# Two slots of a streamed grouped projection share one block of pixels and one store

## The chip, the cores and the metric

The kernel runs on one core of a Trainium2 chip. The time is device microseconds of one execution of the whole program. Three runs of the kernel before took 476.24, 476.40 and 476.92 us, the median is 476.4 us. One more execution was taken with the hardware profiler on; the profile lines in this document come from it.

## The reference

The input is an image of 512 x 512 pixels with 192 channels in bfloat16 (100.7 MB). The channels form 4 groups of 48, and each group has its own 48 x 48 matrix. With a kernel size of 1 there is no neighbourhood: every pixel is multiplied, group by group, by its group's matrix.

```python
H = W = 512; G = 4; Cg = 48; C = 192; k = 1
xg = xp.reshape(B, H, W, G, Cg)
out = out + jnp.einsum('bhwgc,gcd->bhwgd', xg, w[0, 0])
return out.reshape(B, H, W, C)
```

So 262,144 pixels of 384 bytes are read once and written once, and each byte takes part in very little arithmetic.

## The kernel before

**Columns and slots.** Pixels lie in SBUF (the on-chip memory of 128 partitions) as "columns": one column is one pixel of 192 channels in each of the 128 partitions. The input ring `xin` and the output ring `xout` each hold 256 columns. The work is cut into slots of 64 columns, each a block of 128 x 64 pixels that is contiguous in DRAM: partition p gets 64 pixels in a row, that is 24,576 contiguous bytes. `plan_pieces` (L79) makes the list. Slot 0 is cut into pieces of 8, 24 and 32 columns (`HEAD`). Slots 6 and 22 (`SHARED_AT`) are "shared": they fill only some of the partitions, 16 rows by SyncE's queue and 44 rows by GpSimd's queue. The last piece has 4 columns.

**Groups and pairs.** Four columns are a group, two groups a pair. For each group TensorE transposes six 128 x 128 blocks from `xin` into PSUM (`transposes`, L250), VectorE copies the transposed blocks of a whole pair to SBUF (L311), TensorE multiplies them with a block-banded weight matrix `wt` (`matmuls`, L264), and ScalarE casts the 128 x 768 result from PSUM into `xout` (L346). TensorE works one pair ahead with its transposes. There are 529 groups, 16 to a full slot.

**Loads.** SyncE issues them (L234), piece by piece in order. Before a piece it waits until TensorE has finished with the part of the ring that the piece will overwrite (`groups_before`, L180, from the counter `mm_done`). With a ring of four slots the load for a slot is issued when the slot four places earlier is about consumed. GpSimd issues its share of the shared slots, and it also passes each load's landing on to TensorE: it waits for the load's semaphore and raises `ready` (L217 to L219), on which TensorE waits before the first transposes of a piece (L253).

**Stores.** ScalarE issues them from a list made ahead of time (L135 to L146). An entry says which piece, which of its columns, and the group at which it ends. A full slot is one store of 64 columns; in the last nine slots (`LATE`) it is two of 32 columns, and the last but one slot is cut into 24, 16, 12 and 12. ScalarE issues a store after the cast of the second group behind the entry's last one (L347: the entry's end must be smaller than the group just cast). Before it casts a group into a place of `xout` that was used 64 groups earlier, it waits for the store that took that place's old contents (`wait_stored`, L342, found through `store_of`).

```python
for g in range(NG):
    if g >= OUT_COLS // 4:
        wait_stored(store_of[g - OUT_COLS // 4])
    wq.wait(mm_done, g + 1)
    ...
    while todo and todo[0][3] < g:
        store()
```

**Who waits for whom.** TensorE's matmuls wait for ScalarE's casts to free the PSUM buffers (`o_left`, L268) and for VectorE's copies (`e_left`, L265). ScalarE waits for TensorE (`mm_done`) and for stores. SyncE waits only for TensorE.

**DMA engines.** A transfer of all 128 partitions is spread over the core's 16 DMA engines, 8 partitions to an engine. Loads, stores and GpSimd's transfers are in three different queues of the same 16 engines.

Of the kernel before, what the change touches and what calls it, by code (L numbers as in the profile page):

```python
# [11 lines left out]
C = GROUPS * CG  # L12
# [12 lines left out]
SLOT = 64  # L25
# [4 lines left out]
LAST_PARTS = (24, 16, 12, 12)  # L30
LOOP = IN_COLS // 4
SHARED_AT = (6, 22)
SYNC, POOL = 0, 1
SHARED = ((0, 16, 4, SLOT, SYNC), (52, 44, 11, SLOT, POOL))
AHEAD = IN_COLS // SLOT - 2
# [5 lines left out]
class Waiter:  # L41

    def __init__(self, eng):
        self.eng = eng
        self.seen = {}
# [14 lines left out]

class Piece:

    def __init__(self, i, slot, g0, size, shares, pix):
        self.i, self.slot, self.size = i, slot, size
        self.at = {IN_COLS: 4 * g0 % IN_COLS, OUT_COLS: 4 * g0 % OUT_COLS}
        self.g0, self.g1 = g0, g0 + size // 4
        self.full = shares is None
        self.blocks = []
        for (r0, rows, parts, cols, queue) in shares or ((0, 128, 1, size, SYNC),):
            self.blocks.append(Block(r0, rows, parts, cols, queue, pix))  # L70
            pix += rows * cols
        self.pix_end = pix
        assert size % 4 == 0 and all(at + size <= cols for cols, at in self.at.items())
# [5 lines left out]
def plan_pieces(npix):  # L79
    few = sum(rows * cols for _, rows, _, cols, _ in SHARED)  # L80
    at = list(SHARED_AT)
    if npix < len(at) * few + 128 * SLOT * (1 + at[-1]):
        at = []
    cols = (npix - few * len(at)) // 128
    assert cols % 4 == 0
    pieces, g, pix, n = [], 0, 0, 0
    while cols:
        if n in at:
            parts = [(SLOT, SHARED)]
        elif n == 0 and cols >= SLOT:  # L90
            parts = [(s, None) for s in HEAD]
        else:
            parts = [(min(SLOT, cols), None)]
        for s, shares in parts:
            pieces.append(Piece(len(pieces), n, g, s, shares, pix))
            cols -= 0 if shares else s
            g, pix = pieces[-1].g1, pieces[-1].pix_end
        n += 1
    assert pix == npix
    return pieces  # L100


def bass_standalone__grouped__vision_kernel(nc, x, w, out):
# [3 lines left out]
    assert npix % 512 == 0, "the pixel count must be a multiple of 512"  # L107

    pieces = plan_pieces(npix)
    piece_of = {g: p for p in pieces for g in range(p.g0, p.g1)}  # L110
    NG = pieces[-1].g1
# [12 lines left out]
    def transfers(ap, ring, p, queue, c0=0, c1=None):  # L124
        at = p.at[ring.shape[1] // C]
        for b in p.on(queue):
            px = ap[b.pix:b.pix + b.rows * b.cols, :]
            e0, e1 = c0, min(c1 or b.cols, b.cols)
            if b.parts == 1:
                view = px.rearrange("(p i) n -> p (i n)", p=b.rows)[:, e0 * C:e1 * C]  # L130
            else:
                view = px.rearrange("(c a i) n -> a c (i n)", a=b.parts, c=b.rows // b.parts)
            yield b, view, ring[b.r0:b.r0 + b.rows, (at + e0) * C:(at + e1) * C]

    stores = []  # L135
    for p in pieces:
        late = pieces[-1].slot - p.slot
        half = p.size // 8 * 4
        parts = (p.size,)
        if p.full and p.size == SLOT and late < LATE:  # L140
            parts = LAST_PARTS if late == 1 else (p.size - half, half)
        c = 0
        for n in parts:
            stores.append((p, c, c + n, p.g0 + (c + n) // 4))
            c += n
# [4 lines left out]
    with ExitStack() as es:  # L150
# [34 lines left out]
        def _(gp):  # L185
# [13 lines left out]
            def pool_dmas(p, ap, ring, inward, done):  # L199
                for b, dram, sbuf in transfers(ap, ring, p, POOL):  # L200
                    turn = (b.engine - cursor[0]) % 16
                    if turn:
                        few = xf[0:turn, 0:128].rearrange("p (a b) -> p a b", a=2)[:, :, 0:32]
                        gp.dma_start(cur[0:turn, turns[0]], few).then_inc(cur_sem, 16)  # L204
                        turns[0] += 1
                    gp.dma_start(*((sbuf, dram) if inward else (dram, sbuf))).then_inc(done, 16)  # L206
                    cursor[0] = (b.engine + b.parts) % 16
# [20 lines left out]
        @block.sync  # L228
        def _(sp):
            wq = Waiter(sp)  # L230
            for p in pieces:
                wq.wait(mm_done, groups_before(p))
                for _, dram, sbuf in transfers(xf, xin, p, SYNC):
                    sp.dma_start(sbuf, dram).then_inc(ld_sem[p.i], 16)  # L234
# [88 lines left out]
        def _(act):  # L323
# [4 lines left out]
            def store():  # L328
                i = len(stores) - len(todo)
                p, c0, c1, g1 = todo.pop(0)  # L330
                for _, dram, sbuf in transfers(of, xout, p, SYNC, c0, c1):
                    act.dma_start(dram, sbuf).then_inc(st_sem[i], 16)
# [49 lines left out]
```

## Time and profile before

| what | value |
|---|---|
| median of three runs | 476.4 us (476.24 to 476.92) |
| the profiled execution | 476.13 us, of which the span from first to last instruction is 474.0 us |
| TensorE matmul busy | 437.0 us (92%) |
| ScalarE busy | 398.3 us (84%), of which 529 casts of 802 ns on average |
| VectorE busy | 254.1 us (54%) |
| mean rate of all DMA over the span | 425 GB/s (201.53 MB) |
| loads of 64 columns | 30 of 3072 KB on SyncE's queue, 35.7 us from issue to landing (median) |
| stores of 64 columns | 22 of 3072 KB on ScalarE's queue, 33.2 us from issue to landing (median) |
| stores of 32 columns | 15 of 1536 KB, 33.9 us (median) |

The first table of a profile page gives for each engine how long it was busy, its share of the span and how many instructions it ran. The row DMA cuts the span into 40 slices and gives in tenths how busy the 16 DMA engines were on average. A line of a DMA queue names the queue, how many packets it moved, how many MB, and what share of the time of 16 engines these packets took. In the list of waits a line reads: who waited, for whom, microseconds in total, how many times, the longest. In an engine's order of time a line gives start, duration, engine, line of the kernel and operation; an engine's name with a q is its instruction queue, which issues DMAs.

### The profile page before, as it was taken

Reading aid. Unit: us, or ns where it says so; the run is one execution under the profiler, and the core shown is the slowest. Engines: PE = TensorE matmul, PEld = TensorE weight load, DVE = VectorE, ACT = ScalarE, POOL = GpSimd, SP = SyncE. Lnnn points to the kernel's source line nnn. Section 1 sums busy time; section 2 is a strip of 40 time slices with the busy share of each in tenths; the row PEclk is TensorE's granted clock in tenths of the full one; section 3 lists DMA queues with packets and bytes.
Section 4 is the critical chain, followed back from the end, with each engine's and each line's share of the span. In section 5 each row is a group of like instructions: output and inputs, shape, how many; then the busy total and the mean of one; then the engine's idle time right before and its main releaser. Section 6 shows DMA issues by size and latency. Waiting matters only on the chain.

```text
span 474.0 us, 14050 instructions
## 1 busy us (share of the span) xinstructions
PE 437.0 (92%) x6358; PEld 394.0 (83%) x6358; DVE 254.1 (54%) x266; ACT 398.3 (84%) x530; POOL 5.9 (1%) x16
## 2 busy tenths in 40 slices
PE   5999999999999999998889859999999999999970
PEld 5898889888898989887779759898889888898850
DVE  2555655555655555564555525655555555655530
ACT  2899989998999989998788848999889998989870
POOL 1001000000000000000000000000000000000000
PEclk9999999999999999999999989999999999999995
DMA  8999999999999999999999999999999999999997
GB/s 360 401 413 442 427 427 431 429 429 429 425 429 432 431 431 429 435 433 431 429 432 431 433 436 431 433 431 431 431 430 433 430 423 430 438 421 427 427 425 331
DMA packets 11981, 201.53 MB, mean 425 GB/s; under 512 B 1744, under 2 KB 2000, under 8 KB 2640
## 3 DMA queue, kind: packets, MB, share of 16 engines
q10 hardware_dynamic: 6584, 98.52, 48.7%
q1 hardware_dynamic: 4936, 98.50, 48.7%
q0 software_dynamic: 448, 4.33, 2.2%
q8 instruction: 8, 0.13, 0.1%
q14 instruction: 5, 0.04, 0.0%
HBM read 100.68 MB, written 100.66 MB: 425 GB/s over the span
## 4 chain that ended last, share of the span: by engine, by line
PE 63%; DMA 31%; issue 1%; ACT 1%; SPq 0%; POOLq 0%; ACTq 0%
PE o_ps L275 37%; PE xT_ps L260 26%; DMA xin<-in_x_dram 23%; DMA out_dram<-xout 9%; ACT xout L346 1%; SPq L234 0%; POOLq L219 0%; ACTq L51 0%
## 5 line engine op out<-in xcount | busy, mean ns | idle before, releaser
L346 ACT CAST xout<-o_ps 128x768 bf16<-128x768 f32 x529 | 397.0, 802 | 60.7 <-PE o_ps L275 50.5
L311 DVE COPY xT_sb<-xT_ps 128x1536 bf16<-128x1536 bf16 x265 | 253.4, 956 | 198.6 <-PE xT_ps L260 198.6
L275 PE MATMUL o_ps<-wt,xT_sb 128*128 128x144 bf16 (+1 forms) x3174 | 294.7, 234 | 5.6 <-ACT xout L346 1.4
L275 PEld LDWEIGHTS o_ps<-wt,xT_sb 128*128 128x128 bf16 x3174 | 213.3, 98 | 45.5 <-ACT xout L346 30.6
L260 PE MATMUL xT_ps<-ident,xin 128*128 128x128 bf16 x3174 | 223.3, 221 | 12.4 <-POOLq L219 11.1
L260 PEld LDWEIGHTS xT_ps<-ident,xin 128*128 128x128 bf16 x3174 | 191.8, 99 | 15.3 <-POOLq L219 12.6
L204 POOL DMA_DIRECT2D cur<-in_x_dram x4 | 2.3, 584 | 321.2 <-PE o_ps L275 161.4
L246 PE MATMUL o_ps<-w_sb,esel 48*128 48x48 bf16 x10 | 0.6, 209 | 4.4 <-DMA w_sb<-in_w_dram 4.4
L246 PEld LDWEIGHTS o_ps<-w_sb,esel 48*128 48x128 bf16 x10 | 0.5, 111 | 4.3 <-issue 4.3
L305 DVE CAST wt<-o_ps 128x480 bf16<-128x480 f32 x1 | 0.7, 658 | 5.0 <-PE o_ps L246 5.0
L346 ACT ACT_TABLE_LOAD x1 | 1.3, 1283 | 1.3 <-PEq L367 1.3
L206 POOL DMA_DIRECT2D xin<-in_x_dram x2 | 1.1, 564 | 0.0
L206 POOL DMA_DIRECT2D out_dram<-xout x2 | 1.1, 559 | 0.0
L190 POOL TENSOR_SCALAR_AFFINE_SELECT esel<-esel 48x272 bf16<-48x272 bf16 x1 | 0.4, 403 | 0.0
L187 POOL MEMSET esel<- 48x272 bf16 x1 | 0.3, 317 | 0.3 <-POOLq L367 0.3
L194 POOL TENSOR_SCALAR_AFFINE_SELECT ident<-ident 128x128 bf16<-128x128 bf16 x1 | 0.3, 282 | 0.0
L188 POOL MEMSET ident<- 128x128 bf16 x1 | 0.2, 198 | 0.0
L367 POOL MEMSET const-float32-0.0<- 128x1 f32 x1 | 0.1, 99 | 0.3 <-issue 0.3
L367 POOL MEMSET const-bfloat16-1.0<- 128x1 bf16 x1 | 0.1, 102 | 0.0
L367 POOL MEMSET const-uint8-127<- 128x1 uint8 x1 | 0.1, 102 | 0.0
L367 POOL MEMSET const-float32-1.0<- 128x1 f32 x1 | 0.1, 99 | 0.0
## 6 DMA issues: line engine op xcount, KB each, us to landing
xin<-in_x_dram SPq DMA_DIRECT2D x30, 3072.0 KB, 35.7
out_dram<-xout ACTq DMA_DIRECT2D x22, 3072.0 KB, 33.2
out_dram<-xout ACTq DMA_DIRECT2D x15, 1536.0 KB, 33.9
out_dram<-xout ACTq DMA_DIRECT2D x2, 1152.0 KB, 17.7
xin<-in_x_dram POOLq DMA_DIRECT2D x2, 1056.0 KB, 19.8
out_dram<-xout POOLq DMA_DIRECT2D x2, 1056.0 KB, 19.3
xin<-in_x_dram SPq DMA_DIRECT2D x1, 1536.0 KB, 8.9
xin<-in_x_dram SPq DMA_DIRECT2D x3, 384.0 KB, 3.2
```

Of the source, the lines that this page charges most:

```text
L187: gp.memset(esel[:], 1.0).then_inc(p0_sem, 1)
L190: gp.affine_select(out=esel[:], in_=esel[:], pattern=[[-1, ECOLS]], compare_op=AluOpType.is_equal, fill=0.0, base=ESHIFT, channel_multipli ...
L194: gp.affine_select(out=ident[:], in_=ident[:], pattern=[[-1, 128]], compare_op=AluOpType.is_equal, fill=0.0, base=0, channel_multiplier=1) ...
L204: gp.dma_start(cur[0:turn, turns[0]], few).then_inc(cur_sem, 16)
L206: gp.dma_start(*((sbuf, dram) if inward else (dram, sbuf))).then_inc(done, 16)
L246: last = pe.matmul(o_ps[:, NOB - 1, col:col + CG], lhsT=esel[:, s0:s0 + 128], rhs=w_sb[:, g, :], start=True, stop=True, skip_group_check=True)
L260: last = pe.transpose(xT_ps[:, g % NXP, i * 128:(i + 1) * 128], xg[:, i * 128:(i + 1) * 128], ident[:])
L275: last = pe.matmul(o_ps[:, v % NOB, c0_:c1_], lhsT=xs[:, i * 128:(i + 1) * 128], rhs=wt[:, WOFF[tc]:WOFF[tc] + (c1_ - c0_)], start=(tc == ...
L305: dve.tensor_copy(wt[:], o_ps[:, NOB - 1, 0:WCOLS]).then_inc(wc_sem, 1)
L311: dve.tensor_copy(xT_sb[pair % NXS][:, 0:n * 2 * UC].rearrange("p (g c) -> p g c", g=n), xT_ps[:, b0:b0 + n, 0:2 * UC]).then_inc(e_left, 1)
L346: act.copy(dst, o_ps[:, v % NOB:v % NOB + 2, 0:UC]).then_inc(o_left, 1)
L367: nc = _bacc.Bacc("TRN2", target_bir_lowering=False, num_devices=1)
```

## The change

Slots 2 to 5 and 8 to 21 are taken two by two. The two slots of a couple no longer are two blocks of 128 x 64 pixels, but share one block of 128 x 128 pixels: partition p holds 128 pixels in a row (49,152 contiguous bytes in DRAM). The first slot's load takes the first 64 of every partition's pixels, the second slot's load the last 64, so that a load's rows still have 24,576 bytes but lie 49,152 bytes apart in DRAM. The two slots are neighbours in `xin` and `xout`, in halves of the ring. They are stored together, by one transfer of 128 columns whose rows are 49,152 contiguous bytes on both sides. This store takes the place of two in ScalarE's list, and its end is that of the second slot. All other pieces stay as they were. On the other engines the instructions and their order stay the same; on ScalarE nine DMA issues go, and the waits for stores are nine fewer.

```diff
+DOUBLE = (2, 4, 8, 10, 12, 14, 16, 18, 20)
...
-    def __init__(self, i, slot, g0, size, shares, pix):
+    def __init__(self, i, slot, g0, size, shares, pix, off=0, width=0):
...
+        self.double = False
...
-        for (r0, rows, parts, cols, queue) in shares or ((0, 128, 1, size, SYNC),):
+        for (r0, rows, parts, cols, queue) in shares or ((0, 128, 1, width or size, SYNC),):
...
+        elif n in DOUBLE and cols >= 2 * SLOT:
+            for off in (0, SLOT):
+                pieces.append(Piece(len(pieces), n + off // SLOT, g, SLOT, None, pix, off, 2 * SLOT))
+                pieces[-1].double = True
+                g = pieces[-1].g1
+            cols -= 2 * SLOT
+            pix = pieces[-1].pix_end
+            n += 2
+            continue
...
-            e0, e1 = c0, min(c1 or b.cols, b.cols)
+            e0, e1 = c0, c1 or p.size
             if b.parts == 1:
-                view = px.rearrange("(p i) n -> p (i n)", p=b.rows)[:, e0 * C:e1 * C]
+                view = px.rearrange("(p i) n -> p (i n)", p=b.rows)[:, (p.off + e0) * C:(p.off + e1) * C]
...
     for p in pieces:
+        if p.double and p.off:
+            continue
+        if p.double:
+            p = Piece(p.i, p.slot + 1, p.g0, 2 * SLOT, None, p.blocks[0].pix)
```

More of the change, by code (lines that the diff above doesn't have):

```diff
@@ L61 @@
 class Piece:
-    def __init__(self, i, slot, g0, size, shares, pix):
-        self.i, self.slot, self.size = i, slot, size
+    def __init__(self, i, slot, g0, size, shares, pix, off=0, width=0):
+        self.i, self.slot, self.size, self.off = i, slot, size, off
         self.at = {IN_COLS: 4 * g0 % IN_COLS, OUT_COLS: 4 * g0 % OUT_COLS}
```

## The prediction

> **What bounds the kernel now.** I read the page first (busy shares, the slices, the DMA queues), then the waits, then the DMA view in three windows, and last ACT's order of time around its store issues.
>
> ```profile
> span 474.0 us, 14050 instructions
> PE 437.0 (92%) x6358; PEld 394.0 (83%) x6358; DVE 254.1 (54%) x266; ACT 398.3 (84%) x530; POOL 5.9 (1%) x16
> DMA  8999999999999999999999999999999999999997
> q10 hardware_dynamic: 6584, 98.52, 48.7%
> q1 hardware_dynamic: 4936, 98.50, 48.7%
> q0 software_dynamic: 448, 4.33, 2.2%
> ```
>
> q1 carries SP's loads, q10 ACT's stores, q0 POOL's transfers. With 0.1% of instruction fetches the shares add up to 99.7%: on average an engine has a packet in work for 472.6 of 474.0 us. PE at 92% looks almost as full, but PE is the faster of the two. ACT's order of time shows its store issues while nothing starves:
>
> ```profile
> 116.08 0.33 ACTq L332 DMA_DIRECT2D out_dram<-xout  x1
> 129.26 0.34 ACTq L332 DMA_DIRECT2D out_dram<-xout  x1
> 142.38 0.34 ACTq L332 DMA_DIRECT2D out_dram<-xout  x1
> ```
>
> A slot (16 groups) is computed in 13.1 to 13.2 us. Its transfers take longer, as the DMA view of 130 to 190 us (only whole 64-column loads and stores), of 366 to 416 us (stores halved to 32 columns) and of 440 to 460 us (such stores, no loads) shows:
>
> ```profile
> DMA packets 1189, 25.89 MB, mean 431 GB/s; under 512 B 135, under 2 KB 135, under 8 KB 135
> q10 hardware_dynamic: 595, 13.05, 50.7%
> q1 hardware_dynamic: 593, 12.83, 49.7%
> ...
> q1 hardware_dynamic: 613, 13.35, 62.1%
> q10 hardware_dynamic: 615, 8.16, 38.3%
> ...
> DMA packets 783, 8.56 MB, mean 428 GB/s; under 512 B 87, under 2 KB 87, under 8 KB 87
> q10 hardware_dynamic: 782, 8.54, 100.7%
> ```
>
> First window: 100.4% of 16 engines' 60 us is 963.8 us; less 135 semaphore packets at 0.009 us (their time in the packet records), over 1053 data packets: 0.914 us for one row of 24,576 bytes. An engine has 8 of a slot's 128 rows, so a slot costs it 16 x 0.914 = 14.6 us, load and store. DMA therefore sets the pace, and what PE gains per slot it later waits. The middle window shows how an engine shares itself: 613 packets of one queue to 615 of the other, though the stores' rows are half as long, so the bytes go 62 to 38. The queues take turns by packet, not by byte. The last window shows that one queue alone keeps the engines full.
>
> ```profile
> ACT xout L346 <- PE o_ps L275: 50.5, 133, 6.8
> PEld xT_ps L260 <- POOLq L219: 12.6, 7, 5.1
> ACT xout L346 <- DMA out_dram<-xout: 1.7, 2, 1.3
> ```
>
> The 12.6 us behind POOL's "ready" are waits for loads (7 times, to 5.1 us). ACT hardly ever waits for a store: 1.7 us.
>
> **The change, part by part.**
>
> *Loads.* Same count, rows, bytes, issue waits; only the pitch of the rows in DRAM is 49,152 instead of 24,576 bytes. No load here has a pitch of twice its row, but the late stores have: halves of 12,288 bytes in rows 24,576 apart. 440 to 460 us gives 322.2 us less 87 x 0.009, over 695 packets: 0.4625 us, and two of them are 0.925, 0.011 above one long row. So a pitch of two rows costs no more than the extra packet. I take 0; ends: nothing gained (an engine is no quicker than 0.914 in any stretch), and 1.2% lost, that same 0.011 of 0.925 charged to pitch: 1.6 us on 18 slots x 8 x 0.914 = 131.6.
>
> *Stores.* Eighteen stores of 64 columns become nine of 128: per engine 144 packets of 24 KB become 72 of 48 KB. What a packet costs beside its bytes is that 0.011 us by the windows; by the medians of the packet records (0.460 for 12 KB, 0.912 for 24 KB) it is 0.008. I take 0.009: a 48 KB packet takes 1.82 us, and 72 x 0.009 = 0.65 us goes. Nine semaphore packets go too: 9 x 0.009 = 0.08. Together 0.73 us, on the path because the engines are never free. Ends: 0, and 72 x 0.011 + 0.08 = 0.87. The nine issues that ACT drops (0.34 us each, 3 us) are beside the path, under DMA.
>
> The Trainium skill, "DMA: Bandwidth & Descriptors", section "Bandwidth", gives a transfer a fixed cost of about 2 us and advises batching; nine transfers fewer would by that be an estimated 18 us. Here that latency lies under other transfers, as the 99.7% shows, so the trace does not bear it out; it is the last rival.
>
> *The first half waits.* A pair's first slot is stored 13.1 us later. No work is lost by this if the engines have loads meanwhile. In 190 to 260 us a load lands 45.3 us after its issue (median), three loads deep; in 95 to 200 us a store lands after 30.8, two deep. Taking one store of 14.6 us out of the mix leaves both the loads and the rest of the last store. Cover gone, it costs up to 13.1 us a pair, but only if no load is outstanding.
>
> *The out ring.* xout holds 256 columns, now four parts in two halves. A pair's store is issued behind the second cast of the next slot and must have landed 31 casts later, before the ring is reused: 31 x 0.82 (13.1/16) = 25.4 us, where one slot's store had 47 casts, 38.5 us, for its 30.8. What a pair needs: turns by packet, 8 x (1.82 + 0.914) = 21.9 us with loads always in between; plus what issue and landing take, 3.2 us for a 384 KB load into idle queues less 8 x 0.12 for its packets, 2.2. That is 24.1 us: it fits by 1.3. When loads hold PE to 14.6 us a slot there are 28.3. If ACT does wait, every later cast is queued behind it, PE's matmuls behind ACT's counter, and SP's next load and POOL's shared transfers behind PE's. Still nothing is lost while DMA has something queued: the last cast ends near 460.3 us and the last store lands at 473.6; a last store alone would need about 5, so a delay of PE up to some 8 us is hidden.
>
> *Loads beside a pair's store* get a third of an engine: 21.9 us for a load instead of 14.6, then 7.3 alone when the store is through. Over a pair that is 29.2 for two loads and two stores, as now, and the ring of four slots has taken landings of 49.0 us. Cost 0.
>
> **Sum.** 476.13 (the profiled execution, 474.0 of span and 2.1 around it) less 0.73 is 475.40. The median of the runs, 476.4, is 0.27 above that execution: 475.7, which is 0.15% less than 476.4.
>
> **Rivals.**
>
> *The 48 KB row goes out as two packets of 24 KB.* Then turns are one to one: 16 x 2 x 0.914 = 29.2 and 2.2 is 31.4 us against 25.4, ACT waits 6 us for each of nine pairs, and nothing is saved on packets. Unstalled, the casts (first at 9.3 us in ACT's order of time, then 33 slots) would end at 9.3 + 33 x 13.1 = 442; with 9 x 6 on that 496, and 5 for the last store 501. The floor is the 474 of DMA. Loads that run dry speed up the stores, so I take the middle, about 487. For it: no row here is longer than 24,576 bytes. Against: each length from 3,072 to 24,576 went out as one packet. It decides as soon as rows are cut. The Trainium skill's "DMA: Bandwidth & Descriptors", section "Queues, rings and completion order", has a contiguous run moved by one descriptor and cuts only rows longer than 64 KiB, which speaks against this rival; no run yet shows a 48 KB row.
>
> *Whole packets, but the store lands late.* If a pair's landing exceeds 27.2 us, then with two casts (1.6) and the issue (0.4) before the next store a pair takes more than 29.2, and loads run dry in the gap. At 28.5 us it is 1.3 x 9 = 11.7, less the 8 hidden: 479.4. For it: POOL's queue takes a third turn beside slots 4-5 and 20-21, and the margin is 1.3. Against: once loads have caught up, the store gets the whole engine.
>
> *The fixed part of each transfer comes out.* Nine times the 2.2 us above, 20 us: about 456. Against: no idle DMA between 2 us and 471 for it to come from.
>
> **How the numbers follow.** About 0.2%, 0.95 us, is what a measurement of this kernel can tell from no change, so the border of "faster" is 475.45. Forecast 0.76; two packets 0.13; late landing 0.10; fixed cost 0.01. The forecast's own range is 474.9 to 476.6: a saving of 0 to 0.87, the 1.6 of pitch against it, and the spread of the three runs (476.24 to 476.92). It lies close to the border: of its 0.76, 0.28 falls faster, 0.45 same, 0.03 slower. With the fixed cost faster is 0.29; with 0.01 of the late landing same is 0.46; the rest of the rivals makes slower 0.25. The range reaches to 479.4, so that only the two packets, the fixed cost and the forecast's edges are out, 2 in 10.
>
> **What would show it.** Right: store packets of 49,152 bytes (1152 data packets fewer on q10), about 1.82 us each; between a pair's store and its landing some 24 to 27 us; bytes on q10 to q1 about two to one while both run; DMA still 9 in all slices but the ends; ACT's wait for stores under 20 us in total. Wrong: stores' packets as many as now, ACT waiting for DMA 6 us at each pair and slices of DMA below 9 after 140 us; or load packets well above 0.92 us, which would be the pitch.

## The result, and the profile after

The changed kernel takes 489.55 us (median of six runs, 485.35 to 492.24) against 476.65 us before (six runs, 475.88 to 476.97). The ratio is 1.0262, 95% interval 1.024 to 1.0285: by the ratio, slower by 12.5 us. The forecast was 475.7, its range 474.9 to 479.4. The profiled execution took 489.66 us, 13.5 more than that of before. Of 48 more executions of the kernel before, taken beside the experiments, seven were slow runs of 489 to 498 us; these and one run of the cut at 112 and 16 columns stay out of every ratio below, and as no trace of the seven was kept, whether the kernel before can lose its time in the same way is open.

From the page of the changed kernel: span, busy times, DMA's share and rate in 40 slices, the DMA queues (packets, MB, share) and the issues (count, KB each, median us to landing):

```profile
span 487.6 us, 14032 instructions
PE 443.0 (91%) x6358; PEld 401.4 (82%) x6358; DVE 254.0 (52%) x266; ACT 398.8 (82%) x530; POOL 5.9 (1%) x16
DMA  8999999999999999999999999999999999999995
GB/s 356 416 401 432 438 452 407 395 448 379 429 429 432 419 391 419 448 401 403 425 431 399 416 405 431 411 425 433 391 401 431 432 426 429 429 429 424 427 399 234
q1 hardware_dynamic: 4936, 98.50, 48.3%
q10 hardware_dynamic: 5288, 98.52, 48.2%
out_dram<-xout ACTq DMA_DIRECT2D x9, 6144.0 KB, 28.0
```

The bytes are those of before, and q10 has 1296 packets fewer: 1152 of data and 144 semaphore packets. So the change did what it says, and a row of 48 KB goes out as one packet. DMA is still shown busy in every slice, but the slices from 70 to 350 us move 379 to 452 GB/s, where before they moved 425 to 436. This is the same row of the page of before:

```profile
GB/s 360 401 413 442 427 427 431 429 429 429 425 429 432 431 431 429 435 433 431 429 432 431 433 436 431 433 431 431 431 430 433 430 423 430 438 421 427 427 425 331
```

The engines are not idle, they are slower. The DMA view of 60 to 400 us shows by how much. Of before:

```profile
DMA packets 7053, 146.48 MB, mean 431 GB/s; under 512 B 970, under 2 KB 970, under 8 KB 970
```

and of the changed kernel:

```profile
DMA packets 5491, 142.23 MB, mean 418 GB/s; under 512 B 797, under 2 KB 797, under 8 KB 797
```

In these 340 us the changed kernel falls behind by 4.25 MB, 9.9 us at 431 GB/s. Up to 60 us both kernels move the same (24.51 and 24.53 MB), so the other 3.6 us are at the end. There ScalarE's order of time has its last issue of stores, first of before, then of the changed kernel:

```profile
459.51 1.18 ACTq L332 DMA_DIRECT2D out_dram<-xout  x2
...
478.29 1.42 ACTq L347 DMA_DIRECT2D out_dram<-xout  x2
```

The issue comes 18.8 us later, and the transfers after it end about 9 us later instead of 14. That is more than the "8 us" for which the prediction had seen cover.

The list of waits of the changed kernel (who waited for whom, us in total, times, longest):

```profile
ACT xout L361 <- DMA out_dram<-xout: 16.7, 7, 6.2
PE o_ps L290 <- ACT xout L361: 13.7, 9, 5.4
PEld xT_ps L275 <- POOLq L234: 12.3, 3, 6.0
```

ScalarE now waits for stores, 16.7 us instead of 1.7. ScalarE's order of time shows where (start, duration, and in brackets the idle time and what ended it):

```profile
175.48 0.80 ACT L361 CAST xout<-o_ps 128x768 bf16<-128x768 f32 x1 [2.48 <-DMA out_dram<-xout]
175.49 0.34 ACTq L347 DMA_DIRECT2D out_dram<-xout  x1
...
202.64 0.80 ACT L361 CAST xout<-o_ps 128x768 bf16<-128x768 f32 x1 [1.24 <-DMA out_dram<-xout]
202.65 0.34 ACTq L347 DMA_DIRECT2D out_dram<-xout  x1
```

The landing of one pair's store releases the cast, and the next pair's store is issued at once: between the two the store queue has nothing.

The trace also holds every DMA packet with its start, size and duration. These records, put together by size (queue, bytes, packets, median, mean and longest in us):

```
before   loads   24576  3872   0.912  0.917  1.405
         stores  24576  2848   0.912  0.916  1.325
changed  loads   24576  3872   0.912  0.937  2.081
         stores  49152  1152   1.815  1.884  3.039
```

The median is what the prediction had (1.82), the mean is not. On one engine packets follow each other within 4 ns, so the records can be strung into engines (where two packets end together, which one goes on is a choice). Four engines from 172 to 206 us (L a load packet, S a store packet, l' and s' semaphore packets; the duration stands only behind packets that took longer than usual):

```
172.3 s' L L L L l' L L L1.32 L1.50 S L S L S L S L S l' S L S L S L s' L s' L L L L L1.77
172.3 L s' L L L l' L L1.54 L1.82 L1.16 S L S L S L S L S l' S L S L S L L L L L l' L1.12
172.6 s' L L L l' L L L L1.29 S L S L S L L S1.95 L S1.96 L S1.96 L S1.96 l' S1.97 L s' L L L L L
172.7 s' L L l' L L L L1.17 L1.30 S L S L S L S l' S L S L S L S L s' L s' L L L L L
```

and three that at 150 us write the store before:

```
150.2 l' L S L S L S L S2.43 L S2.55 L S2.50 L S2.52 L S
150.3 l' L S L S L S L S2.43 L S2.51 L S2.47 L S2.52 L S
150.4 l' L S L S L S L S1.97 L S2.65 L S2.50 L S2.51 L S
```

Two kinds of lost time: the last loads before a store starts in an empty queue take up to twice their time, on all engines at once; and some engines fall into long stores of about 2 to 2.6 us instead of 1.82. All kernels below can be accounted for in this way. "Base" prices each packet by the usual time of its size (the median), "longer" is what packets took above that, "idle" the rest, each per engine in us. The three add up to the landing of the last bytes, to 0.1 us. Records of packets overlap by 2 to 3 us an engine in every kernel of the table, so "idle" is too small by that and serves only to compare the rows:

| kernel | end of the last packet | base | longer | idle |
|---|---|---|---|---|
| before | 473.2 | 469.6 | 2.9 | 0.8 |
| changed | 486.7 | 468.9 | 13.1 | 4.8 |
| layout alone | 473.1 | 469.6 | 2.7 | 0.9 |
| layout, both stores late | 473.3 | 469.6 | 2.8 | 1.0 |
| one store of two blocks | 487.6 | 469.5 | 8.5 | 9.5 |
| five pairs apart | 495.3 | 469.2 | 13.2 | 12.8 |
| five pairs in a row | 483.2 | 469.2 | 7.2 | 6.9 |
| cut at 124 and 4 | 490.8 | 469.6 | 11.1 | 10.1 |
| loads in halves | 477.1 | 470.9 | 5.6 | 0.5 |
| stores in halves | 481.6 | 470.9 | 6.3 | 4.5 |
| one load for a pair | 479.7 | 468.9 | 5.9 | 5.0 |

The 0.7 us that the prediction counted on is in the second column: 468.9 against 469.6. Of the changed kernel's additional 10.2 us in "longer", 4.9 lie in loads, 4.7 in stores and 0.6 in GpSimd's transfers. Of what the loads lose, 3.7 us are in packets that began while the store queue was empty and less than 4 us before a store's first packet. Of the additional idle time 3.4 us are at the end. So the whole is 0.7 us saved, 10.2 lost in longer packets and 4.0 lost in idle time: 13.5.

### The profile page after: what moved, and what is told of

Its sections match the earlier page's. It is cut to its first block, busy times and chain, and to the rows that moved or that the text cites. A ratio compares the mean times of both kernels' runs of the same rounds, so it can differ in the third digit from the quotient of the medians.

```text
span 487.6 us, 14032 instructions
## 1 busy us (share of the span) xinstructions
PE 443.0 (91%) x6358; PEld 401.4 (82%) x6358; DVE 254.0 (52%) x266; ACT 398.8 (82%) x530; POOL 5.9 (1%) x16
## 4 chain that ended last, share of the span: by engine, by line
DMA 50%; PE 46%; ACT 1%; issue 1%; SPq 0%; ACTq 0%; POOLq 0%
DMA out_dram<-xout 29%; PE o_ps L290 27%; DMA xin<-in_x_dram 21%; PE xT_ps L275 19%; ACT xout L361 1%; SPq L249 0%; ACTq L52 0%; POOLq L234 0%
## 5 line engine op out<-in xcount | busy, mean ns | idle before, releaser
L290 PE MATMUL o_ps<-wt,xT_sb 128*128 128x144 bf16 (+1 forms) x3174 | 297.8, 236 | 18.0 <-ACT xout L361 13.7
L290 PEld LDWEIGHTS o_ps<-wt,xT_sb 128*128 128x128 bf16 x3174 | 216.8, 99 | 57.4 <-ACT xout L361 30.8
L275 PE MATMUL xT_ps<-ident,xin 128*128 128x128 bf16 x3174 | 227.1, 223 | 13.0 <-POOLq L234 11.6
L275 PEld LDWEIGHTS xT_ps<-ident,xin 128*128 128x128 bf16 x3174 | 195.6, 100 | 15.0 <-POOLq L234 12.3
```

The source lines that it names most:

```text
L275: last = pe.transpose(xT_ps[:, g % NXP, i * 128:(i + 1) * 128], xg[:, i * 128:(i + 1) * 128], ident[:])
L290: last = pe.matmul(o_ps[:, v % NOB, c0_:c1_], lhsT=xs[:, i * 128:(i + 1) * 128], rhs=wt[:, WOFF[tc]:WOFF[tc] + (c1_ - c0_)], start=(tc == ...
```

## The experiments

**The layout alone.** Each slot of a pair stores its own half of the block, as soon as it is done.

```diff
-        if p.double and p.off:
-            continue
-        if p.double:
-            p = Piece(p.i, p.slot + 1, p.g0, 2 * SLOT, None, p.blocks[0].pix)
```

> Theories on the 13 us. Pitch: loads and stores with rows 49,152 bytes apart are slower in DRAM, which shows as packets of 24 KB above 0.912 us. Grain: one store of 128 columns, issued late and landing as a whole, leaves the store queue empty in between and makes ScalarE wait. Length: it is the 48 KB packet itself that upsets the engines. This kernel has the changed layout, but stores each slot by itself as soon as it is done, with packets of 24 KB. Pitch expects the whole loss, 485 to 490 us, and load packets near 0.937 us on average. Grain and length expect the time of before, 476 to 477 us.

Measured: 476.39 us, ratio 1.0002 (0.9992 to 1.0012). From its page:

```profile
span 473.9 us, 14050 instructions
q10 hardware_dynamic: 6584, 98.52, 48.7%
q1 hardware_dynamic: 4936, 98.50, 48.6%
```

The shares of both queues are those of before to 0.1%. A row pitch of 48 KB costs nothing; the theory of the pitch is out.

**One store of two blocks.** The layout of before, and one transfer for two slots with two rows of 24 KB in each partition.

```diff
+                px = ap[b.pix:b.pix + 2 * b.rows * b.cols, :]
+                view = px.rearrange("(h p i) n -> p h (i n)", h=2, p=b.rows)
...
+        if p.full and p.slot - 1 in DOUBLE:
+            continue
+        if p.full and p.slot in DOUBLE:
+            stores.append((p, 0, 2 * SLOT, p.g0 + 2 * SLOT // 4))
+            continue
```

> The layout of before, with two slots stored by one transfer of 2 x 24 KB per partition, issued when the second is done. Pitch and length expect the time of before, 476 to 477 us. Grain expects worse than the change: taking turns one to one the store needs 16 x 2 x 0.914 = 29.2 us and some 5 us around it against a window of 25.4, so ScalarE waits some 9 us for each pair, and the whole takes 490 to 500 us.

Measured: 490.26 us, ratio 1.0286 (1.0248 to 1.0324). The list of waits, and a stretch of 10 us with its engines' busy times, clock, DMA share and GB/s:

```profile
ACT xout L357 <- DMA out_dram<-xout: 30.7, 6, 7.3
```

```profile
145.00:155.00 10.00, 9.89 (x150) 9.02 (x148) 5.94 (x7) 9.20 (x13) 0.00 (x0) 1.00 0.60 226
```

The joint landing alone, without a long row, is enough for the same loss, as the next kernel confirms, which differs from this one in sending the same rows as two transfers with a landing each. Here ScalarE waits longer in all, and the loads run ahead until the ring is full. In the 10 us shown the last pair's store has landed, the next pair is not done, and there is nothing to move: DMA is busy 60% of them, while TensorE works.

**Both stores late.** The layout of before, two stores for a pair, both issued when the second slot is done, each with its own landing.

```diff
-            stores.append((p, c, c + n, p.g0 + (c + n) // 4))
+            stores.append((p, c, c + n, p.g0 + (c + n) // 4 + (SLOT // 4 if p.full and p.slot in DOUBLE else 0)))
```

> The layout of before, two stores of 64 columns for each pair, but both issued when the second slot is done, each with its own semaphore. The first lands after some 20 us of its 25.4, the second has another slot's time. Pitch and length expect 476 to 477 us. Grain, if it is the landing as a whole that counts, expects 476 to 478; if it is the empty store queue in between (the late first half), it expects 482 to 490 us and load packets slowed after each issue.

Measured: 476.63 us, ratio 1.0001 (0.9991 to 1.0012). That the first half waits 13 us for the second costs nothing.

**The same on the changed layout.**

> The same two late stores, on the changed layout: beside the change only the packet's length and the joint landing are gone. Pitch expects 485 to 490 us. Length expects 476 to 478. Grain expects the same as for the kernel with two late stores on the layout of before, within 1 us. If pitch and lateness add up, this one is above both the kernel with the layout alone and the one with late stores alone.

Measured: 476.30 us, ratio 1.0007 (0.9981 to 1.0032). Its list of waits:

```profile
ACT xout L357 <- DMA out_dram<-xout: 18.7, 11, 2.3
PE o_ps L286 <- ACT xout L357: 14.2, 12, 1.9
```

ScalarE waits for stores 18.7 us, longer than in the changed kernel (16.7), and the time is that of before. So the sum of these waits is not what costs; the longest of them is 2.3 us here and 6.2 there. The step of the prediction that hid them behind DMA held, as long as the second store is still in the queue when the first lands. This kernel differs from the changed one in two things, the packet's length and the joint landing.

**Five pairs instead of nine**, first with single slots between them, `DOUBLE = (2, 8, 12, 16, 20)`:

> The changed kernel with five pairs instead of nine, at slots 2, 8, 12, 16 and 20, with at least two slots stored singly between them. If what costs is that the store queue runs empty after a pair's store, while the next pair is still being computed, then a single store that follows within 13 us keeps the queue filled: 476 to 477 us, and packets of 48 KB at 1.82 us. If each long store costs by itself, 5/9 of 13 us: 483 to 484 us.

Measured: 494.92 us, ratio 1.0379 (1.0347 to 1.0410), the slowest of all kernels that do the whole work. Then one behind the other, `DOUBLE = (12, 14, 16, 18, 20)`:

> Also five pairs, but at slots 12, 14, 16, 18 and 20, one behind the other. Empty queue: four stretches without a store between pairs, so about half of the loss, 481 to 485 us, clearly above five pairs apart. Cost by the long store itself: the same as five pairs apart, 483 to 484 us.

Measured: 484.72 us, ratio 1.0164 (1.0138 to 1.0190). The order is the opposite of what the theory of the empty store queue expected, and a fixed price for each long store fails as well. The waits of the kernel with five pairs apart show what happens there:

```profile
PEld xT_ps L275 <- POOLq L234: 30.3, 9, 7.4
ACT xout L361 <- DMA out_dram<-xout: 7.0, 2, 4.4
```

TensorE waits for loads, 30.3 us, and ScalarE hardly for stores. The reading is that in taking turns eight long store packets let eight load packets by, one slot's load for two slots of stores. With single stores queued behind a pair's, the loads have no stretch to themselves in which to catch up; from slot 11 to slot 20 a load lands 44 to 51 us after its issue, TensorE runs out, and then both queues run out. That the loads were late and the queues empty is in the trace (12.8 us idle); that the turns are the reason is argued.

**The pair's store cut in two**, at 124 and 4 columns and at 112 and 16, issued together at the pair's end.

```diff
+        if p.size == 2 * SLOT:
+            parts = (124, 4)
...
-            stores.append((p, c, c + n, p.g0 + (c + n) // 4))
+            stores.append((p, c, c + n, p.g1 if p.size == 2 * SLOT else p.g0 + (c + n) // 4))
```

> The changed kernel with each pair's store cut into 124 and 4 columns, issued together at the pair's end, each with its own semaphore. The long rows have 47,616 bytes, and their landing lets ScalarE go on as late as before (8 x (1.76 + 0.914) plus 5, some 26 to 27 us against 25.4), so ScalarE waits as in the changed kernel. But eight short packets follow, which take turns with loads and keep the store queue filled some 8 us longer. Empty queue: 476 to 478 us. Length of packets, or ScalarE's waits: 485 to 490 us.

> The same cut at 112 and 16 columns: long rows of 43,008 bytes land after some 8 x (1.59 + 0.914) plus 5, 25 us, so that ScalarE waits little, and the store queue is filled some 9 us longer. Empty queue: 476 to 477 us. ScalarE's waits: clearly below the cut at 124 and 4. Length of packets: near that of the changed kernel, 484 to 489 us.

Measured: 494.14 us, ratio 1.0350 (1.0285 to 1.0416), and 488.47 us, ratio 1.0236 (1.0203 to 1.0269). Neither keeps the time of before. By the packet records of the cut at 124 and 4, the store queue has no gap over 1.8 us from 70 to 400 us, where the changed kernel has eight of 4 to 9 us, and yet "longer" is 11.1 us. So a filled store queue alone does not bring the time back. The test was not as clean as planned: in the queue the next pair's long part has to wait for that short part, which takes turns with loads, and it lands later still (in the cut at 124 a long part lands 29.9 us after its issue, median).

**Unequal turns without long rows.** Loads of the same 18 slots cut into halves of 32 columns; then stores.

```diff
+HALVED = (2, 3, 4, 5) + tuple(range(8, 22))
...
+                for c0, c1 in ((0, 32), (32, 64)) if p.slot in HALVED else ((0, None),):
+                    for _, dram, sbuf in transfers(xf, xin, p, SYNC, c0, c1):
```

> The kernel of before, with each load of slots 2 to 5 and 8 to 21 cut into two of 32 columns on the same semaphore. Rows are 12 KB then, 16 packets for loads to 8 for stores, so that taking turns by packet gives stores two thirds of the bytes, as in the changed kernel, but with no long row and no joint landing; a store lands after some 8 x (0.914 + 0.46) plus 5, 16 us, of 38.5. Theory of turns: stores overtake, the store queue empties at each slot, loads land late, TensorE waits for them, and packets lengthen when the store queue starts again: 480 to 490 us, of which 1.3 us (18 x 8 x 0.009) for the packets. Theory of joint landing: 477 to 478 us. Theory of the 48 KB row: 477 to 478 us.

```diff
-        if p.full and p.size == SLOT and late < LATE:
+        if p.full and p.size == SLOT and (late < LATE or p.slot in HALVED):
```

> The mirror: loads as before, stores of slots 2 to 5 and 8 to 21 cut into two of 32 columns, each as soon as it is done. Turns give loads two thirds of the bytes. Theory of turns in its plain form (any inequality costs) expects 480 us and more. If it is only starved loads that cost, loads are early here, stores lag and are waited for by ScalarE, DMA always has something queued: 477 to 479 us. Joint landing and the 48 KB row: 477 to 478 us.

Measured: 480.09 us, ratio 1.0091 (1.0058 to 1.0123), and 482.80 us, ratio 1.0146 (1.0061 to 1.0232). Both are slower by more than the 1.3 us that the packets cost, in "longer" and, for the stores, in idle time. Turns of unequal bytes cost something in either direction, 4.3 and 7.0 us by the ratios, of which 1.3 us is the packets; the interval of the second reaches from 2.9 to 11 us. For both that is less than the change costs.

**The streams: what a long packet costs.** No arithmetic and no dependence but four transfers in flight on each queue (three for loads of 48 KB). Each stream ran once.

```diff
+            for i in range(nl):
+                if i >= 4:
+                    sp.wait_ge(ld[i - 4], 16)
+                sp.dma_start(xin[:, c:c + SLOT * C], px).then_inc(ld[i], 16)
...
+            for i in range(ns):
+                if i >= 4:
+                    act.wait_ge(st[i - 4], 16)
+                act.dma_start(px, xout[:, 0:WIDE * C]).then_inc(st[i], 16)
```

> No arithmetic: 32 loads of 64 columns (24 KB rows, up to four in flight) and 16 stores of zeros of 128 columns (48 KB rows, up to four in flight), after one memset of xout; nothing else waits. The output is not the reference's. It shows the price of 48 KB packets beside 24 KB ones in queues that never run empty. Theory of the 48 KB row: store packets well above 1.82 us (1.88 on average in the changed kernel, single ones to 3), loads and stores together above 468 us. Theory of turns, or of joint landing: 1.82 to 1.83 us, 467 us for all transfers (16 x 8 x 1.82 plus 32 x 8 x 0.914) with the last third loads alone.

> The same with 32 stores of 64 columns. The output is not the reference's. All theories: packets of 0.912 to 0.917 us, 468 us for all transfers. It is the yardstick of the streams with 48 KB rows.

> The streams again, but only the 16 stores of 128 columns (48 KB rows), no loads. The output is not the reference's. If it is the long row that is slow in itself, packets near the 2.36 us that they took beside loads. If it takes a load beside it, 1.82 us.

> Streams of 32 loads of 64 columns and 16 stores of 128 columns, where the two halves of a row stand four columns apart in xout, so that a row of 48 KB, still contiguous in DRAM, goes out as two packets of 24 KB. The output is not the reference's. Places in DRAM and bytes per store are those of the streams with 48 KB rows. If the length of the packet is what is slow, 0.912 to 0.92 us a packet; if the places in DRAM are, near 1.18 us (half of 2.36).

> Streams of 32 loads of 64 columns and 21 stores of 96 columns (rows of 36,864 bytes; 32 columns of the output are not written). The output is not the reference's. At the price of short rows a packet takes 1.364 us (36,864/24,576 x 0.904 plus 0.008). If the price grows with length beyond 24 KB, in between, some 1.5 us; if 48 KB is a case by itself, 1.36 to 1.38 us.

> The mirror of the streams: 16 loads of 128 columns (48 KB rows, three in flight) beside 32 stores of 64 columns (24 KB rows). The output is not the reference's. If a long packet of either kind is slow beside short ones of the other queue, load packets near 2.36 us; if only long stores are, 1.82 us.

All six by the DMA view of 40 to 200 us (MB and rate of all, then each queue's packets, MB and share of 16 engines' time). Stores of 48 KB beside loads of 24 KB:

```profile
DMA packets 1768, 57.48 MB, mean 359 GB/s; under 512 B 208, under 2 KB 208, under 8 KB 208
q10 hardware_dynamic: 883, 38.29, 72.3%
q1 hardware_dynamic: 885, 19.19, 27.9%
```

Stores of 24 KB beside loads of 24 KB:

```profile
DMA packets 3168, 69.21 MB, mean 433 GB/s; under 512 B 352, under 2 KB 352, under 8 KB 352
q10 hardware_dynamic: 1584, 34.60, 50.3%
```

Stores of 48 KB alone:

```profile
q10 hardware_dynamic: 1584, 69.21, 100.3%
```

The 48 KB rows sent as two packets, beside loads:

```profile
q10 hardware_dynamic: 1535, 35.37, 51.6%
```

Stores of 36 KB beside loads:

```profile
q10 hardware_dynamic: 1248, 40.70, 60.0%
```

Loads of 48 KB beside stores of 24 KB:

```profile
q1 hardware_dynamic: 1044, 45.81, 66.1%
```

A queue's share of 16 x 160 us, over its bytes in rows, gives the price of a row: 38.29 MB are 779 rows of 48 KB in 1851 us, 2.38 us each. The others in the same way: 0.915 us (24 KB), 1.82 (48 KB alone), 0.918 (each half of 48 KB), 1.39 (36 KB) and 1.82 (48 KB loads). So in the streams one combination is slow: a store packet of 48 KB next to loads, at 2.38 us instead of 1.82, 31% more, and it draws the whole rate down to 359 GB/s. It is not the length by itself, not the bytes' places in DRAM, and not long packets of the loads. The combination is not all of it, though. By the packet records 99% of the long stores in that stream took over 5% longer than the shortest of 1.815 us; in the changed kernel, where they take turns with the same loads, 17% did, and the median is 1.82. What the stream has that the kernel mostly has not is not shown.

**One load for a pair**, the mirror of the change: long loads with a joint landing, stores one by one.

```diff
+                if p.double:
+                    wq.wait(mm_done, groups_before(pieces[p.i + 1]))
+                    both = Piece(p.i, p.slot, p.g0, 2 * SLOT, None, p.blocks[0].pix)
+                    for _, dram, sbuf in transfers(xf, xin, both, SYNC):
+                        sp.dma_start(sbuf, dram).then_inc(ld_sem[p.i], 16)
+                    continue
```

> The mirror of the change: the same layout, the two slots of a pair loaded by one transfer of 128 columns (48 KB rows), issued when both places in the ring are free, and stored one by one as soon as each is done. Loads now move by two thirds, land as a whole some 27 us after their issue (8 x (1.82 + 0.914) plus 5) against 26 us of work that TensorE has left, so that TensorE waits at each pair as ScalarE does in the changed kernel; but long loads beside short stores took 1.82 us in the streams. If the slow long store packets made the loss, 476 to 479 us. If the joint landing and the stretches with one queue empty made it, 484 us and more.

Measured: 481.52 us, ratio 1.0089 (1.0061 to 1.0118). From its page:

```profile
span 480.6 us, 14041 instructions
xin<-in_x_dram SPq DMA_DIRECT2D x9, 6144.0 KB, 26.9
```

It lies between the two expectations: a third of the loss is there, 4.3 us. But this kernel is not free of slow long packets, as the streams had made likely. By the packet records 10% of its long loads take over 5% longer, up to 3.39 us, and of the 5.9 us in "longer" 3.4 lie in them. So it does not separate the joint landing from the long packets, and it does not show that the other two thirds are slow long stores; the kernel with one store of two blocks has no long store and loses 13.6. No run has long rows without a joint landing.

## Why the prediction was wrong

Two steps failed. The price of a long store packet, which was to take 0.7 us away, added 4.9 us an engine. And the joint landing of a pair, which was priced at nothing because "still nothing is lost while DMA has something queued", went with longer loads (4.9 us an engine) and a delayed end (4.0 us more idle time, 3.4 of them there). That the second is enough by itself is shown by the kernel with one store of two blocks, which loses 13.6 us with rows of 24 KB.

- *What bounds the kernel.* Right: with the order of stores and the layout altered, and ScalarE kept waiting 18.7 us, the time stays within 0.1% as long as the engines' packets keep their price.
- *Loads at a pitch of two rows: 0.* Right, 1.0002 (0.9992 to 1.0012).
- *Stores: a 48 KB packet takes 1.82 us, 0.73 us goes.* This is the first step that failed. The row goes out as one packet, 1152 of them, and 1.82 is right alone and at the median. Beside loads the streams show 2.38 us, and in the changed kernel the mean is 1.884: 72 x 0.069 = 5.0 us an engine added (4.9 without the rounding), not 0.65 taken away. The step drew a line through 12 KB and 24 KB and went on along it to a size that no row of the trace had; its upper end, "0", allowed for no loss. The Trainium skill ("DMA: Bandwidth & Descriptors", section "Why a DMA increments its semaphore by 16 and not by 1", not the section that the prediction names) has one descriptor move one contiguous run. The trace agrees: 49,152 bytes in one packet.
- *The first half waits: no cost.* Right: two late stores, 1.0001 (0.9991 to 1.0012).
- *The out ring: 24.1 us against 25.4, "it fits by 1.3".* Wrong: 28.0 us at the median. The 2.2 us for issue and landing came from a load into idle queues, where the first packet followed its issue by 1.0 us. Behind running loads a pair's first store packet came 3.3 to 3.9 us after its issue in eight of nine cases, and engines with slow stores end late.
- *"Still nothing is lost while DMA has something queued."* This is the second step that failed, and it is half right. It holds for the waits themselves. It does not hold for what follows a joint landing: the store queue is empty for 3.2 to 9.4 us before each of the nine pairs' stores, and in the 3 us before the next store's first packet the load packets grow by up to 0.8 us an engine, with the engines busy by their records. Such load packets hold 3.7 of the 4.9 us that loads lose over the run. The cover of "some 8 us" at the end was overrun by casts that end 19 us later.
- *Loads beside a pair's store: cost 0.* Not tested by itself. In the changed kernel TensorE waits for loads no more than before (12.3 us against 12.6); the five pairs apart, where it waits 30.3 us for loads, speak against a cost of 0 in general.
- *The rivals.* "Two packets of 24 KB" named 487 us, close to the result, for a reason that did not occur: the packets are whole. What happened is nearest to "whole packets, but the store lands late", with a landing at 28.0 us, beyond its 27.2. But its own sum gives (28.0 - 27.2) x 9 = 7.2 us at that landing, all of it under the 8 hidden, so it would have forecast no loss: it knew neither the slow packets nor the slower loads.
- *The signs.* Most of what the prediction named as signs of being right came: 1152 data packets fewer, 1.82 us at the median, DMA at 9 in all slices but the ends, ScalarE's wait for stores under 20 us (16.7). Only the landing did not (28.0 us against 24 to 27). A median and a busy share do not show packets of which some are slow; the mean and the rate do.
- *Batching.* Larger transfers did not pay: the 0.7 us are there in the base price, and nothing more. The Trainium skill ("DMA: Bandwidth & Descriptors", section "Bandwidth") advises at least 1 MiB for a transfer. The stores of before had 3 MiB, so that advice asked for no merging here. The fixed cost of about 2 us, which the prediction quotes from that section, the page gives in another, "Anatomy of one DMA — SWDGE (gpsimd) path", for transfers that GpSimd issues.

What stays open: how the 12.5 us divide exactly between the slow long stores and the joint landing, since the joint landing alone costs as much and no run has the long rows alone; why a long store beside loads is slow, always in the stream and in 17% of the packets here; and why loads take longer just before a store starts in an empty queue. None of the kernels is faster than before by more than can be measured.

## What to carry to other kernels

When DMA engines are full, merging transfers could here save no more than the packets' fixed cost (0.7 of 474 us), so look first at what the merged transfer does to the queues: how many packets each queue has for the same work, how long a landing the ring allows, and whether a queue runs empty between. Keep one more transfer behind the one whose landing is waited for, and do not go on along a price line to a packet size that no trace has shown in the same company: a stream of nothing but transfers measures it in one run.

## What the runs showed of the hardware that was not expected

- In streams, store packets of 49,152 bytes take 1.82 us alone and 2.38 us when they take turns with loads of 24,576 bytes; loads of 49,152 bytes beside stores of 24,576 take 1.82; stores of 36,864 bytes beside loads 1.39. In the kernels it is not so clear-cut: 17% of the long stores of the changed kernel and 10% of the long loads of its mirror were slow.
- A store issued into an empty queue while loads run moves its first packet 3.3 to 3.9 us later, against 1.0 us for the first load of the program.
- A DMA share of 1.00 need not mean full rate: from 60 to 400 us both kernels show the engines busy throughout, at 431 and at 418 GB/s.
